# One attention step's scores and keys on one pair of banks, in a fused mLSTM and expert kernel

## The chip, the cores and the metric

The kernel runs on one core of a Trainium2 chip. The metric is the device time of one execution in microseconds (us). TensorE is written PE, VectorE DVE, ScalarE ACT, GpSimd POOL and SyncE SP. Scratch memory of the matmul engine (PSUM) has 8 banks of 512 f32 columns by 128 rows.

## The reference

Four sequences, 8 heads, 768 positions, head size 40. A gated recurrence runs over the positions; its output passes a sigmoid gate, a layer norm and a two-layer network with a residual. All in f32.

```python
for t in range(S):
    m_new = np.maximum(f_gate[:, :, t] + m, i_gate[:, :, t])
    f_stab = np.exp(f_gate[:, :, t] + m - m_new)
    i_stab = np.exp(i_gate[:, :, t] - m_new)
    C = f_stab * C + i_stab * einsum('bhd,bhe->bhde', vt, kt)
    n = f_stab * n + i_stab * kt
    h_tilde = einsum('bhde,bhe->bhd', C, qt)
    denom = np.maximum(np.abs(nq), 1.0)            # nq = n . qt
    y[:, :, t] = sigmoid(o_gate) * h_tilde / denom
x = y as (4, 768, 320)
xn = (x - mean) / sqrt(var + 1e-6) * g_ln
out = x + relu(xn @ w_ch1) @ w_ch2                 # 320 -> 1280 -> 320
```

## The kernel before

The recurrence is computed in chunks of 128 positions. There are 6 chunks (c) of 4 sequences (b), so 24 steps, st = 4c + b; two steps make a pair p, and the expert network works on a pair, 256 positions at once. The program is a list of small pieces, and one long text, `ORDER`, says in which order they are issued: every engine takes its own instructions in that order, and a piece waits on its engine for what it reads and for the buffer or bank that it writes. `@` in the order names the banks of a piece. There is no other scheduler.

The pieces of a step, in the order in which they depend on each other:

- Gates of a chunk: `gm`, `gg`, `gate`, `gu` on DVE and POOL make running maxima, the cumulated log forget gates `gc` and the key-side exponents `uu`. `gst` and `gse` store `gc` and its exponential to DRAM (issued from ACT's queue), `G` and `eg` load them back spread over rows (from SP's queue). `gta`/`gca` and `gr`/`gtr`/`gcr` turn `uu` and its exponential into columns, by a transpose on PE and a copy on DVE.
- Weights of scores: in the first chunk `gx` builds the log weights of a step on PE (mask, then a broadcast of `gc`), and `ex` takes the exponential, one activation per head with the key-side term as bias. In later chunks `sel` masks what `G` loaded, and `ex` does the same.
- `S`: scores of 8 heads. From step 4 on, a chunk is two halves of L = 64 positions, and the score matmuls are 64x64 tiles. `P` multiplies the scores by the weights on DVE.
- `km`, `kv`: weighted keys on POOL, and keys times values on PE, one product per half of the rows, each in a bank of its own. `sd`, `sa`, `se`, `st` carry the state: decay to the middle of the chunk (POOL), plus the first half's product (DVE), decay to its end (POOL), plus the second's (DVE).
- `int`: queries (`qm`) times the state, 64x64 tiles; `pv`: weights times values, added in the same bank, with 64x32 tiles. `n1`, `n2`, `n3`, `sq`, `np`, `nx` normalise and gate on DVE, ACT and POOL; `T`, `xh`, `xl` transpose and split into a high and a low part.
- Expert: `m1.p.f.i` is 8 matmuls of 128x128 weights by 256 columns, `hh` and `hl` split the rectified result, `m2.p.f.j` is 6 matmuls of 320 columns, `ob` and `out` finish and store. f runs over 5 blocks of 256 inner columns. The weights come as 11 tiles: `wl` loads, `cA`, `cB`, `cT`, `cH`, `cL`, `cI` convert and split, `cR` copies half rows.
- `fill` is a matmul into bank 7 that nothing reads.

The first pieces and the way to the first expert matmul in the old order:

```
gin ini id g0 wl.1 wl.0 ld.1 fill.513 fill.513 fill.496 fill.496 fill.496 fill.496 fill.256 fill.256 fill.256 fill.256
fill.320 fill.320 fill.320 fill.320 fill.257 fill.257 fill.257 fill.257 cst ld.0 tok.0 gm.0 wl.2 gg.0 ld.2 gate.0 gu.0
...
fill.512 st.3 fill.512 P.3.1 gex.3 gu.3 kv.2@1 gst.2 P.3.0 fill.512 fill.512 st.2 pv.3 gst.3 sel.5 gm.4 gse.2 gta.3@2
fill.512 n1.3 fill.512 gr.3 gca.3 fill.512 cB.5 n2.3 ex.5.0 gtr.3@6 gcr.3 tok.2 cT.3.0 S.5@0@5 ex.5.1 wl.9 n3.2
m1.0.0.0@1 cT.3.1 nx.2 m1.0.0.1 sq.2 n3.3 cR.3 sd.4 cH.3 P.5.0 T.2@2 fill.512 np.2 nx.3 cI.3@3 gse.3 sel.4 xh.2 hh.0.0
```

Of the kernel before, what the change touches and what calls it, by code (L numbers as in the profile page):

```python
# [20 lines left out]
C = 128  # L21
# [3 lines left out]
VA = 41  # L25
# [11 lines left out]
GP = 4  # L37
NE = 4
# [3 lines left out]
BUFS = {'y': 7, 'xt': 2, 'ht': 4, 'wraw': 4, 'w': 5, 'w0': 2, 'qk': 5, 'wt': 3}  # L42

ORDER = """
gin ini id g0 wl.1 wl.0 ld.1 fill.513 fill.513 fill.496 fill.496 fill.496 fill.496 fill.256 fill.256 fill.256 fill.256
fill.320 fill.320 fill.320 fill.320 fill.257 fill.257 fill.257 fill.257 cst ld.0 tok.0 gm.0 wl.2 gg.0 ld.2 gate.0 gu.0
wl.4 cB.1 cA.1 gm.1 cT.1.0 gg.1 tok.1 cA.0 gta.0@0 gx.1@1@2 gca.0 gr.0 cB.0 gate.1 gex.1 gst.1 g8 cT.1.1 S.1@3@4 gse.1
ex.1.1 cT.0.0 gtr.0@5 wl.3 gx.0@0@6 cT.0.1 gu.1 ex.1.0 P.1.1 cH.1 gcr.0 S.0@1@2 P.1.0 ex.0.0 gm.2 gta.1@4 cI.1@5 gca.1
gg.2 ex.0.1 P.0.0 ld.3 int.1@3@4 pv.1 sig.0 P.0.1 km.1 fill.512 int.0@0@1 cH.0 pv.0 n1.1 km.0 n2.1 n3.1 kv.1@6 wl.5
cB.2 gr.1 gx.3@2@3 n1.0 sq.1 n2.0 nx.1 np.1 kv.0@4 cA.2 n3.0 gx.2@0@1 st.1 ex.3.1 cT.2.0 fill.513 cL.0 st.0 ex.3.0  # L50
cB.4 gtr.1@6 S.2@3@4 nx.0 gate.2 ex.2.0 gcr.1 T.0@2 gu.2 fill.513 ex.2.1 P.2.0 fill.512 fill.512 gex.2 cT.2.1 gta.2@6
km.3 G.5 xh.0 int.2@0@1 fill.513 sq.0 P.2.1 cR.0 fill.512 gr.2 ld.5 gm.3 np.0 int.3@3@4 pv.2 cL.1 cR.2 xl.0 sig.1 eg.2
cB.3 gtr.2@5 gca.2 cH.2 n1.2 T.1@2 G.4 gg.3 kv.3@6 gcr.2 n2.2 xh.1 ld.4 cA.3 S.3@0@5 xl.1 cA.4 fill.512 km.2 gate.3
fill.512 st.3 fill.512 P.3.1 gex.3 gu.3 kv.2@1 gst.2 P.3.0 fill.512 fill.512 st.2 pv.3 gst.3 sel.5 gm.4 gse.2 gta.3@2
fill.512 n1.3 fill.512 gr.3 gca.3 fill.512 cB.5 n2.3 ex.5.0 gtr.3@6 gcr.3 tok.2 cT.3.0 S.5@0@5 ex.5.1 wl.9 n3.2
m1.0.0.0@1 cT.3.1 nx.2 m1.0.0.1 sq.2 n3.3 cR.3 sd.4 cH.3 P.5.0 T.2@2 fill.512 np.2 nx.3 cI.3@3 gse.3 sel.4 xh.2 hh.0.0
fill.512 xl.2 S.4@4@6 sq.3 qm.4 hl.0.0 cL.3 T.3@0 ex.4.0 m1.0.1.0@7 gg.4 xh.3 m1.0.1.1 ex.4.1 xl.3 sd.5 gate.4
m1.1.1.0@5 hh.0.1 P.4.0 np.3 gex.4 sig.2 m1.1.0.0@2 hl.0.1 km.4 gst.4 gse.4 m1.1.1.1 km.5 gu.4 m1.1.0.1 hh.1.1 hl.1.1
kv.4@1@3 hh.1.0 cB.9 gm.5 gta.4@0 gr.4 sa.4 qm.5 hl.1.0 int.4@6@7 gca.4 gtr.4@4 pv.4 se.4 gcr.4 gg.5 st.4 kv.5@1@5
n1.4 n2.4 sa.5 int.5@2@3 cL.2 pv.5 se.5 gate.5 cA.5 cT.4.0 gu.5 gex.5 gst.5 cA.9 st.5 m2.1.0.0@0 n1.5 gse.5 n2.5  # L60
m2.0.0.1@4 cT.4.1 m2.1.0.1@6 cT.5.0 cH.4 wl.6 ld.8 gta.5@7 cT.9.0 m2.0.0.0@1 gr.5 cR.1 cL.4 wl.7 gtr.5@5 ld.6 cT.9.1
m2.0.1.1 G.7 cT.5.1 cH.9 ld.7 m2.1.1.1 gcr.5 n3.4 G.6 cH.5 m2.0.1.0 cL.9 nx.4 wl.8 cL.5 sq.4 cB.6 m2.1.1.0 cA.6 gca.5
# [35 lines left out]
out.5.1 sq.16 ld.21 m1.7.2.1 ld.20 hh.7.0 np.16 ld.23 hl.7.0 out.6.1 T.16@6 sel.20 hh.7.2 m1.7.3.1 xh.16 hl.7.2
m1.7.1.0@7 ex.20.1 xl.16 m2.7.0.0@0 hh.7.3 ex.20.0 hl.7.3 m1.7.1.1 sig.9 m1.7.4.0@1 hh.7.1 sel.22 hl.7.1 m1.7.4.1
kv.17@2@5 ex.22.1 m2.7.0.1@4 km.19 sa.17 ex.22.0 km.18 m2.7.1.1 hh.7.4 hl.7.4 m2.7.1.0 m2.7.2.1 int.17@6@7 pv.17 se.17  # L100
S.22@2@3 qm.19 st.17 n1.17 kv.18@1@5 n2.17 m2.7.2.0 P.22.0 sd.19 sa.18 n3.17 m2.7.3.0 sq.17 int.18@6@7 nx.17 np.17
# [22 lines left out]
def mlstm_moe_kernel(  # L124
# [63 lines left out]
    @piece  # L188
    def g0(_=None):
        nc.sync.dma_start(out=g0_sb, in_=gate0)  # L190
# [659 lines left out]
```

## Time and profile before

| | us |
|---|---|
| median of 3 runs | 339.9 (335.12 to 339.96) |
| the profiled execution | 336.42 |
| its span in the profile | 334.6 |
| PE busy | 317.9 (95%) |
| DVE, ACT, POOL busy | 167.8, 149.8, 133.0 |

The span runs from the first to the last instruction of the program; 1.8 us of the profiled execution lie outside it. Busy time counts overlapping instructions once. Most of PE's matmuls are pipelined: the step from one start to the next is shorter than the time of one.

### The profile page before, as it was taken

What the parts mean: (1) busy time and instruction counts of PE and PEld (TensorE: products, weight loads), DVE (VectorE), ACT (ScalarE), POOL (GpSimd) and SP (SyncE); (2) the same over time, 40 slices, a digit from 0 to 9 for tenths busy, and PEclk for the clock granted to TensorE, in tenths of its full rate; (3) what the DMA queues carried; (4) which work ended last, traced back from release to release, by engine and by line L of the source; (5) the groups of instructions that cost most, each with busy time, mean ns of one, the idle gap of its engine ahead of it and who ended that gap; (6) DMA issues with size and microseconds to landing.
All of it is one profiled execution on the core that took longest, in us unless ns stands there. A gap on an engine that the chain in (4) does not pass through costs nothing.

```text
span 334.6 us, 12179 instructions
## 1 busy us (share of the span) xinstructions
PE 317.9 (95%) x5280; PEld 295.2 (88%) x5280; DVE 167.8 (50%) x419; ACT 149.8 (45%) x411; POOL 133.0 (40%) x221
## 2 busy tenths in 40 slices
PE   7899689999999999999998999999999999999995
PEld 4776577999998998999998899989998999999995
DVE  4778457989744524444441644444444624263221
ACT  2897573568544242236356146228128222252120
POOL 5967196355706321642543355344315423010000
PEclk9999899999999999999999999999999999999999
DMA  7998950698045460049970195355045060000011
GB/s 228 314 318 222 278 165 6 173 348 221 4 120 128 135 209 3 4 145 275 260 167 5 39 205 191 100 194 156 4 130 166 4 202 12 2 24 0 21 41 39
DMA packets 16434, 43.98 MB, mean 131 GB/s; under 512 B 2684, under 2 KB 6012, under 8 KB 16380
## 3 DMA queue, kind: packets, MB, share of 16 engines
q1 hardware_dynamic: 15740, 43.03, 44.4%
q8 instruction: 41, 0.67, 0.8%
q10 hardware_dynamic: 640, 0.16, 0.2%
q14 instruction: 13, 0.11, 0.1%
HBM read 38.44 MB, written 4.10 MB: 127 GB/s over the span
## 4 chain that ended last, share of the span: by engine, by line
PE 69%; DMA 10%; DVE 9%; POOL 4%; issue 3%; ACT 2%; SPq 1%; ACTq 0%; DVEq 0%; POOLq 0%
PE banks L600 27%; PE banks L627 10%; PE banks L628 9%; PE banks L629 9%; DMA wraw<-in_w1a_dram 4%; PE banks L490 4%; PE banks L416 3%; DMA w<-gsc 3%; DMA wraw<-in_w_dram 3%; PE banks L378 2%; PE banks L432 2%; DVE w L386 2%; DVE wt L680 2%; DVE wt L684 1%; PE banks L566 1%
## 5 line engine op out<-in xcount | busy, mean ns | idle before, releaser
L627 PE MATMUL banks<-w2h,hh 128*128 128x320 f32 x240 | 77.2, 322 | 1.8 <-DVE w L386 1.8
L628 PE MATMUL banks<-w2l,hh 128*128 128x320 f32 x240 | 74.2, 309 | 0.8 <-DVE w2l L735 0.8
L629 PE MATMUL banks<-w2h,hl 128*128 128x320 f32 x240 | 73.9, 308 | 0.0
L612 DVE SCALAR_TENSOR_TENSOR hl<-banks,hh 128x512 fp32r<-128x512 f32 x60 | 40.8, 689 | 55.2 <-ACT hh L605 55.1
L600 PE MATMUL banks<-xh,w1h 128*128 128x256 f32 x360 | 63.4, 285 | 1.6 <-DVE w L386 1.5
L600 PE MATMUL banks<-xh,w1l 128*128 128x256 f32 x360 | 61.5, 280 | 0.0
L605 ACT ACTIVATE hh<-banks 128x512 fp32r<-128x512 f32 x60 | 35.1, 592 | 50.8 <-PE banks L600 44.7
L600 PEld LDWEIGHTS banks<-xh,w1h 128*128 128x128 f32 x360 | 51.1, 189 | 3.0 <-DVE w L386 1.4
L600 PEld LDWEIGHTS banks<-xh,w1l 128*128 128x128 f32 x360 | 50.7, 190 | 0.0
L627 PEld LDWEIGHTS banks<-w2h,hh 128*128 128x128 f32 x240 | 45.0, 188 | 4.8 <-DVE w L386 2.5
L600 PE MATMUL banks<-xl,w1h 128*128 128x256 f32 x240 | 47.7, 280 | 1.1 <-issue 1.1
L344 ACT ACTIVATE w<-w,ar_sb 128x64 f32<-128x64 f32 x160 | 40.5, 337 | 13.0 <-POOL w L333 13.0
L628 PEld LDWEIGHTS banks<-w2l,hh 128*128 128x128 f32 x240 | 45.1, 188 | 1.3 <-DVE w2l L735 1.3
L629 PEld LDWEIGHTS banks<-w2h,hl 128*128 128x128 f32 x240 | 45.0, 188 | 0.0
L600 PEld LDWEIGHTS banks<-xl,w1h 128*128 128x128 f32 x240 | 36.8, 190 | 0.0
L392 POOL TENSOR_TENSOR qe<-qk,eg 104x512 f32<-104x512 f32 x20 | 25.6, 1283 | 23.4 <-PE banks L416 12.8
L333 POOL TENSOR_SCALAR_AFFINE_SELECT w<-w 64x512 f32<-64x512 f32 x40 | 28.4, 710 | 12.8 <-DMA w<-gsc 11.0
L634 DVE SCALAR_TENSOR_TENSOR y<-banks,rs,y 128x320 f32<-128x320 f32 x24 | 13.2, 550 | 32.4 <-PE banks L629 32.1
L548 ACT ACTIVATE junk<-y,sum 128x320 bf16<-128x320 f32 x24 | 13.3, 555 | 33.0 <-DVE y L534 33.0
L401 POOL TENSOR_TENSOR kp<-tok,ar_sb 128x320 f32<-128x320 f32 x24 | 16.9, 721 | 26.7 <-issue 9.8
L386 DVE TENSOR_TENSOR w<-banks,w 128x512 f32<-128x512 f32 x28 | 19.0, 688 | 15.1 <-PE banks L378 4.2
L573 ACT ACTIVATE xh<-banks 128x384 fp32r<-128x384 f32 x24 | 11.6, 489 | 32.5 <-PE banks L567 32.5
(101 smaller groups left out, 451.9 us busy)
## 6 DMA issues: line engine op xcount, KB each, us to landing
tok<-in_tok_dram SPq DMA_DIRECT2D x12, 968.0 KB
qk<-in_qk_dram SPq DMA_DIRECT2D x24, 416.0 KB
w<-gsc SPq DMA_DIRECT2D x40, 128.0 KB
out_dram<-y SPq DMA_DIRECT2D x24, 160.0 KB
wraw<-in_w_dram SPq DMA_DIRECT2D x5, 640.0 KB
wraw<-in_w1a_dram SPq DMA_DIRECT2D x5, 512.0 KB
eg<-esc SPq DMA_DIRECT2D x10, 256.0 KB
eg<-esc SPq DMA_DIRECT2D x10, 160.0 KB
```

Source lines behind the costliest of these rows:

```text
L333: nc.gpsimd.affine_select(out=v, in_=v, pattern=[[0, H], [1, L]], compare_op=ALU.is_ge, fill=NEG, base=0, channel_multiplier=-1)
L344: nc.scalar.activation(out=w[:, h], in_=ps[:, hh], func=AF.Exp, bias=ar_sb[:, c, 0, b * H + h:b * H + h + 1])
L386: nc.vector.tensor_tensor(out=w, in0=s_t.pop((st, half)), in1=w, op=ALU.mult)
L392: nc.gpsimd.tensor_tensor(out=t, in0=qk_t[st][:, 0], in1=eg_t[p][:, j], op=ALU.mult)
L401: nc.gpsimd.tensor_tensor(out=kp_t[st][:, :DM].rearrange("p (h e) -> p h e", h=H), in0=kn, in1=ar_sb[:, c, 1, b * H:(b + 1) * H].unsqueeze ...
L490: nc.tensor.matmul(Y[x + i:x + i + 32, h], w[x:x + L, h, i:i + 32], tok_t[p][x:x + L, j, h * VA:(h + 1) * VA], start=False, stop=(g == 3), ...
L600: nc.tensor.matmul(ps[:, i], a, x, start=(n == 0), stop=(n == len(ops) - 1))
L605: nc.scalar.activation(out=t, in_=h1_t[p, f], func=AF.Relu)
L612: nc.vector.scalar_tensor_tensor(out=l.rearrange("p a t -> p (a t)"), in0=ps.rearrange("p a t -> p (a t)"), scalar=0.0, in1=t.rearrange("p ...
L627: nc.tensor.matmul(ps, t[:, i, sl], w2h[:, ff], start=(ff == 0), stop=False)
L628: nc.tensor.matmul(ps, t[:, i, sl], w2l[:, ff], start=False, stop=False)
L629: nc.tensor.matmul(ps, l[:, i, sl], w2h[:, ff], start=False, stop=(ff == KF - 1))
```

## The change

1. From step 4 on, `S` also does the key matmuls of `kv`: scores take columns 0 to 255 of two neighbouring banks, the key products columns from 256 on of the same two. `kv` is left for the first four steps alone.
2. Each sequence has two state tiles, used in turn: `se` and `st` write one, `sd` and `int` of that step read the other.
3. `pv` uses 64x64 tiles instead of 64x32 ones: two matmuls per head, on the two diagonal blocks, instead of four.
4. In the first chunk `gx` adds `uu` on PE too (two matmuls of 64 rows by 512 columns), and `ex` is one activation for four heads without a bias. `gta.0` and `gca.0` go. `gr` writes to a tile `rr` of its own.
5. `gst` and `gse` are issued from SP's queue; the gates come in one load per chunk; `w` has 9 buffers for both kinds of weight tile; 24 of 35 `fill`s go; the order is a new one. `sy` is a DVE copy of one element of `int`'s bank, once.

```diff
+UB = 1
+GA = ()
-BUFS = {'y': 7, 'xt': 2, 'ht': 4, 'wraw': 4, 'w': 5, 'w0': 2, 'qk': 5, 'wt': 3}
+BUFS = {'y': 7, 'xt': 2, 'ht': 4, 'wraw': 4, 'w': 9, 'qk': 5, 'wt': 3}
...
+g0 ini id ld.1 gin.1 cst gin.2 fill.513 fill.513 fill.496 fill.496 fill.496 fill.496 fill.256 fill.256 fill.256
+fill.256 fill.320 ld.0 wl.0 gm.0 wl.1 gg.0 tok.0 gate.0 wl.2 g8 gu.0 ld.3 ld.2 gm.1 gg.1 gx.0@0@1 gate.1 gu.1 gst.1
+wl.3 S.0@2@3 cB.0 ex.0.0 gm.2 gin.3 cA.0 gx.1@0@4 ex.0.1 tok.1 cB.1 cA.1 P.0.1 dg cT.0.0 cT.0.1 S.1@1@3 ex.1.0 cT.1.0
+ex.1.1 gg.2 gx.2@0@5 P.0.0 cH.0 P.1.1 P.1.0 gr.0 cT.1.1 sig.0 cL.0 int.0@6@7 pv.0 ex.2.1 cB.2 cH.1 gtr.0@1 int.1@2@3
+pv.1 cA.2 gcr.0 ex.2.0 gx.3@1@4 n1.1 km.0 n2.1 n1.0 km.1 n2.0 G.5 cT.2.0 wl.5 n3.0 S.3@0@5 ex.3.0 n3.1 ex.3.1 cB.3
+S.2@2@3 gex.1 gate.2 nx.0 gse.1 P.3.0 cA.3 cR.2 gu.2 kv.1@1 P.3.1 sq.1 kv.0@4 nx.1 cT.3.0 gin.4 cR.0 T.0@0 cT.3.1 G.6
+int.3@6@7 cI.1@5 xh.0 cT.2.1 cH.3 wl.4 km.3 pv.3 gm.3 st.1 st.0 xl.0 wl.7 km.2 cL.1 kv.3@1 sq.0 P.2.0 sel.5 T.1@0
+P.2.1 kv.2@4 xh.1 wl.6 cA.5 int.2@2@3 pv.2 gg.3 xl.1 G.4 st.3 sig.1 n1.3 cI.3@5 cR.3 n1.2 cH.2 cR.1 n2.3 cB.5 eg.2
+n2.2 m1.0.0.0@1 n3.2 cL.3 tok.2 n3.3 m1.0.0.1 nx.2 cT.5.0 nx.3 T.2@0 m1.0.1.0@7 hh.0.0 cL.2 ld.4 cB.4 xh.2 hl.0.0
...
-    state = [const.tile([104, 4, VA], F32, name=f"state{b}") for b in range(B)]
+    state = [[const.tile([104, 4, VA], F32, name=f"state{b}_{i}") for i in range(2)] for b in range(B)]
...
     def gst(c):
-        nc.scalar.dma_start(
+        (nc.scalar if c in GA else nc.sync).dma_start(
...
-            nc.scalar.activation(out=u, in_=u, func=AF.Exp, bias=gc[k][0:n, x + m - 1:x + m])
+            nc.scalar.activation(
+                out=rr[k][0:BH, x:x + m], in_=uu[k][0:BH, x:x + m], func=AF.Exp, bias=gc[k][0:BH, x + m - 1:x + m]
+            )
...
+        if st < GP and (UB or st >= B):
+            nc.scalar.activation(out=w, in_=ps, func=AF.Exp)
+            return
...
+        if c or UB:
+            for x in range(0, C, n):
+                for z in range(2):
+                    zs, m, hb = slice(64 * z, 64 * z + 64), slice(x, x + n), 64 * z + b * H + 4 * z
+                    mm(ps[z][m], uu[c % 2][zs, m], id_sb[zs, hb:hb + 4].unsqueeze(2).to_broadcast([64, 4, n]),
+                       start=False, stop=False)
...
+        assert at[1] == at[0] + 1
+        s_t[st, 0] = banks[:, at[0]:at[0] + 2, :4 * L]
+        for g in range(4):
+            for j in range(0, C, L):
+                for z in range(2):
+                    r, m = slice(64 * z, 64 * z + D), slice(j, j + L)
+                    nc.tensor.matmul(
+                        banks[m, at[z], g * L:g * L + L], t[r, 1, g, m], t[r, 0, g, m], start=True, stop=True,
+                        skip_group_check=True
+                    )
+        p, j = divmod(st, 2)
+        kf = kp_t[st]
+        nx = 1 if st >= NST - B else 2
         for g in range(4):
             for z in range(2):
+                h, e = g + 4 * z, (g + 4 * z) * D
+                for x in range(nx):
+                    r, o = slice(L * x, L * x + L), 4 * L + g * VA
                     nc.tensor.matmul(
+                        banks[64 * z:64 * z + 64, at[x], o:o + VA], kf[r, e:e + 64],
+                        tok_t[p][r, j, h * VA:(h + 1) * VA], start=True, stop=True, skip_group_check=True,
                     )
...
     def se(st):
         b = st % B
         p, j = divmod(st, 2)
         nc.gpsimd.tensor_tensor(
-            out=state[b], in0=sa_t[st], in1=eg_t[p][:, j, :, C - 1:C].to_broadcast([104, 4, VA]), op=ALU.mult
+            out=state[b][st // B % 2], in0=sa_t[st], in1=eg_t[p][:, j, :, C - 1:C].to_broadcast([104, 4, VA]), op=ALU.mult
         )
...
     def pv(st):
...
-                    for i in range(0, L, 32):
-                        for x in (0, L):
-                            nc.tensor.matmul(
-                                Y[x + i:x + i + 32, h], w[x:x + L, h, i:i + 32],
-                                tok_t[p][x:x + L, j, h * VA:(h + 1) * VA], start=False, stop=(g == 3),
-                                skip_group_check=True,
-                            )
+                    for x in (0, L):
+                        m = slice(x, x + L)
+                        nc.tensor.matmul(
+                            Y[m, h], w[m, h], tok_t[p][m, j, h * VA:(h + 1) * VA], start=False, stop=(g == 3),
+                            skip_group_check=True,
+                        )
```

## Rows read from the trace of the kernel before

**Rows 1.** The page: engine totals, and the granted clock in 40 slices.

```profile
PE 317.9 (95%) x5280; PEld 295.2 (88%) x5280; DVE 167.8 (50%) x419; ACT 149.8 (45%) x411; POOL 133.0 (40%) x221
...
PEclk9999899999999999999999999999999999999999
```

**Rows 2.** Windows: stretch, length, each engine's busy us, then clock, DMA share, GB/s.

```profile
0.00:30.90 30.90, 28.25 (x326) 19.89 (x327) 20.96 (x62) 22.53 (x63) 21.30 (x44) 1.00 0.92 274
30.90:39.00 8.10, 5.13 (x99) 3.13 (x95) 3.94 (x12) 2.70 (x11) 2.86 (x5) 1.00 0.93 244
39.00:46.30 7.30, 6.27 (x68) 5.45 (x63) 4.20 (x12) 5.70 (x19) 4.76 (x9) 0.77 0.94 287
60.00:86.60 26.60, 26.00 (x280) 24.88 (x278) 23.80 (x41) 18.47 (x46) 13.48 (x19) 1.00 0.80 233
```

**Rows 3.** PE's groups by form, the f32 fills of 512 columns.

```profile
L782 PE MATMUL banks<-id_sb 128*128 128x512 f32 x10 | 7.0, 807 | 1.7 <-POOL id_sb L751 1.7
```

**Rows 4.** Timeline of PE, 38 to 47 us: start, length, what, idle before.

```profile
38.11 0.33 PE L295 MATMUL banks<-id_sb,uu 128*128 128x128 f32 x1 [2.97 <-ACT uu L320]
...
38.99 0.62 PE L600 MATMUL banks<-xh,w1h 128*128 128x256 f32 x3
...
43.35 0.41 PE L566 MATMUL banks<-id_sb,xn 128*128 128x128 f32 x2 [1.03 <-DVE w L386]
...
46.27 0.60 PE L600 MATMUL banks<-xh,w1h 128*128 128x256 f32 x3
```

**Rows 5.** The chain of waits from 100 to 104 us: start, length, what.

```profile
100.14 0.61 PE banks L416 x32
100.75 0.73 PE banks L490 x64
101.48 0.62 PE banks L378 x32
102.10 0.45 PE banks L432 x32
102.55 0.34 PE banks L627
102.89 0.14 PE banks L628
```

**Rows 6.** The same chain: a run of nine `m1`, and `kv` with one half.

```profile
117.99 8.19 PE banks L600 x72
...
259.36 0.46 PE banks L432 x16
```

**Rows 7.** Timeline of ACT, its DMA queue (ACTq) included, 34 to 38 us.

```profile
34.77 0.33 ACTq L281 DMA_DIRECT2D gsc<-gc  x1
...
36.50 0.32 ACTq L281 DMA_DIRECT2D gsc<-gc  x1
...
37.47 0.58 ACT L320 ACTIVATE uu<-uu,gc 32x64 f32<-32x64 f32 x2 [2.02 <-DMA w<-gsc]
```

**Rows 8.** DVE's groups by form: count, busy us, mean ns of one, idle before.

```profile
L386 DVE TENSOR_TENSOR w<-banks,w 128x512 f32<-128x512 f32 x28 | 19.0, 688 | 15.1 <-PE banks L378 4.2 <-PE banks L629 4.2 <-POOL w L333 2.0
L524 DVE SCALAR_TENSOR_TENSOR y<-tok,banks 128x320 f32<-128x320 f32 x24 | 11.4, 479 | 0.0
...
L680 DVE SCALAR_TENSOR_TENSOR wt<-wt,wraw 128x512 int32<-128x512 int32 x5 | 3.9, 795 | 0.0
L684 DVE SCALAR_TENSOR_TENSOR wt<-wraw,wt 128x512 int32<-128x512 int32 x5 | 3.6, 743 | 0.0
L307 DVE COPY ar_sb<-banks 128x32 f32<-128x32 f32 x6 | 1.1, 184 | 1.2 <-PE banks L295 1.2
```

**Rows 9.** Who waited for whom: us in total, times, longest.

```profile
POOL state L466 <- PE banks L416: 25.7, 7, 10.4
PE banks L627 <- DVE w L386: 1.8, 3, 0.8
```

**Rows 10.** Timeline of PE, its last matmul.

```profile
330.82 0.30 PE L629 MATMUL banks<-w2h,hl 128*128 128x320 f32 x1
```

More of the change, by code (lines that the diff above doesn't have):

```diff
@@ L48 @@
[L48 to L62, printed above, removed]
@@ L98 @@
[L98 to L101, printed above, removed]
-pv.18 m2.7.4.0 se.18 n1.18 st.18 n2.18 T.17@2 ob.7.0 m2.7.3.1 xh.17 n3.18 m2.7.4.1 xl.17 sq.18 S.21@1@3 nx.18 np.18
@@ new lines @@
+ld.10 hh.1.4 G.9 st.6 cL.10 int.5@0@1 G.10 gtr.2@7 n3.4 sd.7 m2.0.3.1 gcr.2 hl.1.4 km.7 gta.2@7 pv.5 gca.2 gm.4 qm.6
+S.7@6@7 n1.5 n2.5 n3.5 tok.4 int.6@0@1 eg.4 m2.0.4.1 sa.7 sq.5 se.7 nx.5 m2.0.4.0 ob.0.1 nx.4 st.7 sig.3 T.4@3 P.7.0
+m2.1.4.1 sq.4 sel.10 xh.4 T.5@6 m2.1.3.0 xl.4 xh.5 qm.7 gr.3 xl.5 m2.1.4.0 m1.2.1.0@3 sel.9 pv.6 np.2 int.7@6@7 n1.6
+m1.2.1.1 gg.4 ob.1.0 n2.6 m1.2.2.0@2 hh.2.1 n3.6 m1.2.2.1 gate.4 m1.2.0.0@0 hl.2.1 hh.2.2 gu.4 gst.4 out.0.1
+m1.2.3.0@1 gse.3 np.0 ld.13 ld.11 m1.2.3.1 km.8 ob.0.0 G.13 hl.2.2 qm.8 m1.2.0.1 G.12 S.8@2@3 G.15 hh.2.0 sd.8 ex.9.0
@@ new lines @@
+sel.11 hl.2.0 gin.5 pv.7 G.14 m2.2.0.1@5 ex.9.1 n1.7 np.5 n2.7 ex.10.1 m2.2.1.1 tok.5 sd.9 eg.5 sel.8 m2.2.0.0@0 nx.6
+out.0.0 ex.11.0 m1.2.4.0@6 km.9 hh.2.3 m2.2.1.0 ex.8.0 n3.7 hl.2.3 m2.2.2.1 ex.8.1 m1.2.4.1 sq.6 P.8.0 nx.7 m2.2.2.0
+np.6 gm.5 hh.2.4 gg.5 m2.2.3.1 hl.2.4 sa.8 m2.2.3.0 se.8 m2.2.4.1 np.3 T.6@1 m2.2.4.0 sel.12 ob.1.1 xh.6 ob.2.1 T.7@4
+xl.6 S.9@6@7 xh.7 km.10 st.8 ex.10.0 xl.7 np.4 S.10@1@2 sig.4 ob.2.0 int.8@3@4 P.9.0 m1.3.0.0@5 sd.10 gate.5 qm.9 sa.9
+gst.5 sa.10 m1.3.0.1 out.1.1 ld.12 se.9 m1.3.1.0@0 out.2.0 hh.3.0 se.10 ld.15 gex.5 st.10 out.2.1 m1.3.1.1 hl.3.0 G.19
@@ L189, in g0, with g1, gin @@
     def g0(_=None):
-        nc.sync.dma_start(out=g0_sb, in_=gate0)
+        nc.sync.dma_start(out=g0_sb, in_=gate0[0])
     @piece
-    def gin_(_=None):
-        nc.sync.dma_start(out=gin, in_=gates)
+    def g1(_=None):
+        nc.sync.dma_start(out=g1_sb, in_=gate0[1])
+    @piece
+    def gin(c):
+        gin_t[c] = gin_p.tile([BH, 2, C], F32, tag="gin", name="gin")
+        nc.sync.dma_start(out=gin_t[c], in_=gates[:, :, (c - 1) * C:c * C])
     @piece
@@ L368, in S_ @@
         t = qk_t[st]
-        n = C if st < B else L
-        for z in range(2):
-            s_t[st, z] = banks[:, at[z], :4 * n].rearrange("p (h t) -> p h t", t=n)
-        if st >= B:
-            s_t[st, 0] = banks[:, at[0]:at[1] + 1:at[1] - at[0], :4 * L]
+        if st < B:
+            for z in range(2):
+                s_t[st, z] = banks[:, at[z]].rearrange("p (h t) -> p h t", t=C)
+            for g in range(4):
+                for z in range(2):
+                    r = slice(64 * z, 64 * z + D)
+                    nc.tensor.matmul(
+                        s_t[st, z][:, g], t[r, 1, g], t[r, 0, g], start=True, stop=True, skip_group_check=True
+                    )
+            return
@@ L374, in S_ @@
+        assert at[1] == at[0] + 1
+        s_t[st, 0] = banks[:, at[0]:at[0] + 2, :4 * L]
         for g in range(4):
-            for j in range(0, C, n):
+            for j in range(0, C, L):
                 for z in range(2):
-                    r, m = slice(64 * z, 64 * z + D), slice(j, j + n)
+                    r, m = slice(64 * z, 64 * z + D), slice(j, j + L)
                     nc.tensor.matmul(
-                        banks[m, at[z], g * n:g * n + n], t[r, 1, g, m], t[r, 0, g, m], start=True, stop=True,
+                        banks[m, at[z], g * L:g * L + L], t[r, 1, g, m], t[r, 0, g, m], start=True, stop=True,
@@ L383, in P @@
+        kv_t[st] = [
+            banks[:104, a, 4 * L:4 * L + 4 * VA].rearrange("p (g d) -> p g d", g=4) for a in at[:nx]
+        ]
     @piece
     def P(st, half):
-        w = W_t[st][:, half * 4:half * 4 + 4] if st < B else W_t[st].rearrange("p (z g) t -> p z (g t)", z=2)
+        w = W_t[st][half] if st < B else W_t[st].rearrange("p (z g) t -> p z (g t)", z=2)
         nc.vector.tensor_tensor(out=w, in0=s_t.pop((st, half)), in1=w, op=ALU.mult)
@@ L425, in kv @@
         kf = kp_t[st]
-        if st >= B:
-            for g in range(4):
-                for z in range(2):
-                    h, e = g + 4 * z, (g + 4 * z) * D
-                    for x, a in enumerate((at, at2) if at2 is not None else (at,)):
-                        r = slice(L * x, L * x + L)
-                        nc.tensor.matmul(
-                            banks[64 * z:64 * z + 64, a, g * VA:(g + 1) * VA], kf[r, e:e + 64],
-                            tok_t[p][r, j, h * VA:(h + 1) * VA], start=True, stop=True, skip_group_check=True,
-                        )
-            kv_t[st] = ps, None if at2 is None else banks[:104, at2, :4 * VA].rearrange("p (g d) -> p g d", g=4)
-            return
         n = 64 if st < NE else 32
@@ L474, in st_, with sy @@
         if st < B:
-            nc.scalar.activation(out=state[b], in_=ps, func=AF.Copy)
+            nc.scalar.activation(out=state[b][0], in_=ps, func=AF.Copy)
         else:
-            nc.vector.tensor_tensor(out=state[b], in0=ps[1], in1=state[b], op=ALU.add)
+            s = state[b][st // B % 2]
+            nc.vector.tensor_tensor(out=s, in0=ps[1], in1=s, op=ALU.add)
+    @piece
+    def sy(st):
+        nc.vector.tensor_copy(out=jk_sb, in_=Y_t[st][0:1, 0, 0:1])
     @piece
@@ L769, in ini @@
         nc.gpsimd.memset(uu[1], 0.0)
+        for k in range(2):
+            nc.gpsimd.memset(rr[k], 0.0)
+            nc.gpsimd.memset(gc[k][GR:], 0.0)
         for t in kps:
```

179 lines of the change are left out of this document (96 added, 83 removed).

## The prediction

> **What bounds the kernel now.** I read the page first: TensorE (PE) is busy for 95% of the span, at its full clock except in the fifth of the 40 slices [rows 1]. So nearly every microsecond is PE work or a place where PE waits, and I went on with the windows to see where it waits. From 60 us on PE is busy 26.0 of 26.6 us. From 0 to 39 it is busy too, but much of that is `fill`, matmuls that compute nothing [rows 2, 3]. The timeline shows the one big hole: after 2.97 us without work the transpose `gtr.3` runs at 38.11, the first matmul of the expert part (`m1.0.0.0`) at 38.99, then things stop again, and `m1.0.1.0` starts only at 46.27 [rows 4]. From 39 to 46.3 the mean granted clock is 0.77, a mixture of the 2.4 and 1.2 GHz levels, right behind that idle stretch [rows 2]. The rest of the run is expert matmuls with short attention pieces in between; the chain of waits prices each piece from the end of the one before to its own [rows 5, 6].
>
> Why is the start late? ScalarE computes `gr.3`, the input of `gtr.3`, at 37.47. Its queue is in order, and ahead of `gr.3` stand the DMA issues `gst.2` and `gst.3`, which go out only at 34.77 and 36.50 [rows 7]. DMA is 0.93 busy in these 8 us [rows 2]: the issues wait their turn and hold up arithmetic behind them.
>
> **The change part by part.**
>
> *Gate stores on SP's queue, a new opening.* `gst` and `gse` leave ScalarE's queue, so that this stall cannot recur there. Queued behind them on SP are now loads, `cR.2`, `wl.4` and `wl.7` among them; who waits for those is the weight conversion. The first `m1` stands behind 1 gate transpose instead of 8, no scores of step 5 and 11 fills instead of 33. Its last input is `xl.1` on VectorE. In the old run VectorE is through with `xl.1` at 30.9, with 20.96 us busy until then [rows 2]. The new list up to `xl.1` has 2 more `P` (0.69 each) and 2 more `cT` (0.80, 0.74); one `n1` and `n2` less (about 0.8, 0.48 of it in `n2`) and 5 copies less (0.18 each): +1.4 +1.5 -0.8 -0.9 = +1.2 us [rows 8]. At the old density (20.96/30.9 = 0.68) `xl.1` is done at 30.9 + 1.2/0.68 = 32.7; at the density of 60 to 86.6 (23.80/26.6 = 0.89), counted from about 6 us, where the first gates are through, at 29 to 30 [rows 2]. What PE has in between overlaps for the most part. I put the first `m1` at 33.0 (bounds 30 and 36), against 39.0: the old density, for the two lists are nearly the same.
>
> *First exponents whole, with the key-side term added on TensorE.* `ex` of the first four steps becomes one activation for four; ScalarE gains, but VectorE paces the opening. `gx` gets four more instructions per step, 64 rows by 512 columns in f32, on two halves of the array. The nearest row is the f32 fill of 512 columns, 7.0 us for ten [rows 3]: 0.7 us each, in two rounds 1.4 us per step, 5.6 in four steps; 11.2 if they take turns. Of that same form 6 of the 10 are removed, 4.2 us, and 21 other fills: they are the cover. If PE instead of VectorE paced the opening, this edit would cost its own size less the fills; that is inside the bound of 36.
>
> *Scores and keys together.* `S` now issues the key matmuls right behind the scores, on one pair of banks. Their number stays: 32 + 32 instructions, 0.45 us for the keys where the shape does not change on entry, L432 behind L378 [rows 5]. What changes is how often PE goes from the expert shape (128x128) to the attention shape and back. `int`, 32 instructions too, costs 0.61 as the first piece of a visit, 0.15 more; the first `m2` behind a visit costs 0.34 where the next costs 0.14, 0.20 more. That is 0.35 us a visit. Counted in the two orders from the first `m1` on, there are 34 visits before and 29 after: -5 x 0.35 = -1.8 us.
>
> *Values in 64x64 tiles.* The old `pv`, 64 instructions with 64x32 weights, costs 0.73 us behind `int`, and `S` behind it 0.62 instead of 0.46: a change of shape costs 0.16 each time, so `pv` itself is 0.57 [rows 5]. These changes (22 counted between the two small shapes) vanish: -22 x 0.16 = -3.5 us. But the new `pv` has 32 instructions on only two 64x64 tiles at a time, the diagonal blocks of a head. The trace has a like case: in the last four steps `kv` needs one half of its rows, 16 instructions on two tiles, and takes 0.46 us, as much as 32 instructions on four [rows 5, 6]. A round of two costs what a round of four costs, so the new `pv` is 2 x 0.46 = 0.92 us: +0.35 x 20 = +7.0 us. Bounds: 0.46 (a round holds four, as for `int`) and 1.84 (the two tiles take turns). I take 0.92, from the nearest row. In sum the attention pieces get dearer: -1.8 - 3.5 + 7.0 = +1.7 us.
>
> *Two states per row.* `se` no longer waits until `int` has read the old state. GpSimd waited 25.7 us in seven waits for that [rows 9], but PE's own waits do not name it; I count it at nothing, and what it may cost or give with the waits for banks.
>
> *Waits for banks.* PE waits for VectorE's `P` before `m2`, 1.8 us in three waits [rows 9], because scores hold banks that others need. The merged pair is held longer (until `P`, `sa`, `se` and `st` are done), but a step asks for fewer banks. Counted as PE work between a bank's last writer and its next user against VectorE's in-order work up to the last reader, the old order falls short by 0.8 us or more at five places from step 4 on, the new one at one. I take -2 us (0 to -3).
>
> *The middle.* From the first `m1` to `m2.0.2.0` the new order gives PE and VectorE 16.4 us each, because weight conversion, expert work and the first attention steps come together. Two in-order engines with equal loads do not overlap fully: at the density 0.89 VectorE needs 18.4 us, at 0.68 it needs 24. I take +2 (0 to +6).
>
> **The sum.** The old run, as a check: first `m1` at 39.0; 120 `m1` at 8.19/9 = 0.91 and 120 `m2` at 6 x 0.15 make 217.2 [rows 5, 6]; 19 `S`, 20 `kv` and 20 `int` at 0.46 and 20 `pv` at 0.57, 38.5; 22 `T` at some 0.5 (an estimate from the 0.41 of two of its three matmuls [rows 4]), 11.0; gate transposes and `cI`, 1.5; 34 x 0.35 + 22 x 0.16 = 15.4 for visits and shapes. That ends at 322.6. PE ends at 331.1 [rows 10], so 8.5 us are losses, 3.5 of them in the stop before 46.3; 3.5 us follow to the end of the span, and 1.8 lie outside it. The new run: 33.0 + 217.2 + 20 x (3 x 0.46 + 0.92) = 46.0 + 11.0 + 2.0 + 29 x 0.35 = 10.2 makes 319.4. Losses 8.5 - 3.5 - 2 + 2 = 5.0, tail 3.5, outside 1.8: 329.7 us against the profiled 336.4, -2.0%. The median of the runs shown, 339.9, lies 1.0% above that execution; the same step puts the new median near 332.
>
> **Rivals.** *The values are cheaper (323 us).* If the price went by rounds of four, the new `pv` would take 0.46, and 20 x 0.46 = 9.2 us fall away: 320.5, or 323 at the median. Against it stand the 16 instructions on two tiles that are as slow as 32 on four [rows 5, 6]. By rows, 64 instructions in 0.73 us are 11 ns each. The Trainium skill, "TensorEngine Tiling (Array Packing)", section Instruction Overhead, gives some 60 cycles to each matmul, an estimate of 25 ns at 2.4 GHz, by which halving their number would save 0.8 us per `pv`; the rows lie below that already.
>
> *The opening does not move (340 us).* The first `m1` comes at 36 and the middle costs its full 6 us, because SP, which now also waits for gates, delivers weights late, or VectorE keeps the density 0.68: 3 + 4 = 7 us more than the sum, 336.7, or 340 at the median. For it: DMA is over 0.92 busy throughout the opening [rows 2], and `wl.7` waits for a buffer that a conversion must leave. Against it: `xl.1` was done at 30.9 before.
>
> *Values take turns (351 us, slower).* The diagonal blocks of a head sit in different row halves of the array and write the same bank. If PE ran them one after the other, `pv` would be 1.84, +0.92 x 20 = +18.4 us; the kernel gets slower by over 2% from about +0.7 us per `pv` on. Against it: the old `pv` mixes both row halves in one bank as well, at 11 ns an instruction [rows 5]. The Trainium skill, "TensorEngine Tiling (Array Packing)", section Gotcha 1: PSUM Pressure, says that different row tiles cannot access the same bank at once; by that rule this rival is the outcome, and the rows speak against it.
>
> **Chances.** Forecast 0.52, values cheaper 0.15, opening unmoved 0.25, turns 0.08. Two per cent is about what a measurement of this kernel can tell from no change; seen from 339.9 it ends at 333.1. The forecast's own range is 326 to 338, from the bounds 30 to 36, 0 to +6 and 0 to -3, not all at one end, and is split nearly evenly: 0.29 faster, 0.23 same. The cheaper values give 0.15 to faster; the unmoved opening 0.21 to same and 0.04 to slower; turns 0.08 to slower: faster 0.44, same 0.44, slower 0.12. The range takes in the first two rivals and leaves out the third: 320 to 343.
>
> **What would show it.** First `m1` near 33 in the timeline, no hole of 3 us on PE and the clock at 1.0 between 30 and 50; `pv` at 0.92 us for 32 instructions; keys behind scores at 0.45; 29 visits. I am wrong if `pv` is near 0.5 or above 1.2, if the first `m1` starts after 36, or if PE idles for more than 6 us behind it.

## The result and the profile after

The changed kernel takes 323.09 us (median of 4 runs, 322.38 to 324.59), the kernel before 338.38 in the same session (4 runs, 335.12 to 339.96): a ratio of 0.957, interval 0.948 to 0.966, 4.3% faster. The forecast was 332 (-2.3%): its range of 320 to 343 holds the result, the gain is about twice the forecast. Ratios here leave out the executions that took over 1.5% longer than the fastest of their kernel (a few took 500 to 600 us), medians leave out none unless it is said, so the two can differ. The profiled execution took 322.62 us, with a span of 320.8.

The page of the changed kernel, against [rows 1]: TensorE's (PE's) totals, its granted clock in 40 slices, and the queue that brings instructions (transfers, MB, share).

```profile
PE 312.1 (97%) x4628; PEld 297.6 (93%) x4628; DVE 168.0 (52%) x419; ACT 143.7 (45%) x387; POOL 132.2 (41%) x225
...
PEclk9999999999999999999999999999999999999999
...
q8 instruction: 36, 0.59, 0.8%
```

The same windows as in [rows 2], then two later stretches. The 0.77 of the clock is gone, and from 87 us to its last matmul PE is never idle.

```profile
30.90:39.00 8.10, 7.78 (x78) 7.16 (x78) 7.80 (x21) 6.58 (x16) 4.92 (x7) 1.00 0.93 309
39.00:46.30 7.30, 7.00 (x56) 7.03 (x57) 6.53 (x13) 4.51 (x12) 0.66 (x2) 1.00 1.04 265
...
60.00:87.30 27.30, 26.77 (x472) 25.68 (x473) 20.91 (x50) 12.26 (x34) 15.49 (x24) 1.00 0.63 177
87.30:293.80 206.50, 206.50 (x3269) 201.82 (x3269) 93.31 (x252) 88.39 (x255) 80.08 (x134) 1.00 0.37 107
```

PE's timeline, against [rows 4] and [rows 10]: the first expert matmul starts at 32.99 (before 38.99), the only stop of any size up to 54 us is the 0.62 us before 39.30, and the last matmul starts at 317.19 (before 330.82).

```profile
32.68 0.47 PE L762 MATMUL banks<-w1h,ni_sb 128*128 128x256 f32 x1
32.99 0.51 PE L641 MATMUL banks<-xh,w1h 128*128 128x256 f32 x3
...
39.30 0.59 PE L641 MATMUL banks<-xh,w1h 128*128 128x256 f32 x3 [0.62 <-DVE xh L625]
...
317.19 0.31 PE L670 MATMUL banks<-w2h,hl 128*128 128x320 f32 x1
```

The chain of waits, against [rows 5]: L412 scores, L424 keys, L465 `int`, L532 `pv`, L641 `m1`.

```profile
176.43 0.62 PE banks L412 x32
177.06 0.45 PE banks L424 x32
177.51 0.49 PE banks L412 x32
177.99 0.45 PE banks L424 x32
178.44 0.49 PE banks L465 x32
...
181.90 0.61 PE banks L465 x32
182.51 0.93 PE banks L532 x32
```

All that PE itself waits for from 33 us on (us in total, times, longest). Before, the same list from 46.3 us on held seven entries with 6.4 us: the PE line of [rows 9] and those of the second view.

```profile
PE banks L641 <- DVE xh L625: 0.6, 1, 0.6
PE banks L465 <- DVE t L574: 0.5, 1, 0.5
```

```profile
PE banks L600 <- DVE w L386: 1.5, 3, 0.8
PE banks L600 <- issue: 1.1, 1, 1.1
PE banks L628 <- DVE w2l L735: 0.8, 2, 0.5
PE banks L416 <- DVE sa L460: 0.6, 2, 0.4
PE banks L378 <- DVE w L386: 0.4, 1, 0.4
PE banks L490 <- issue: 0.2, 1, 0.2
```

That list names a wait only where the trace shows a releaser. To count everything I took, for each pair of neighbouring forms of PE instruction, the steps from start to start, and called what a step has over the lower quartile of its pair, if that is more than 60 ns, its excess. What remains is work.

| us | before | after | forecast of the difference | measured |
|---|---|---|---|---|
| first `m1` starts | 39.0 | 33.0 | -6.0 | -6.0 |
| work from there to the last matmul | 273.1 | 275.9 | 286.4 - 283.6 = +2.8 | +2.8 |
| excess | 18.8 | 8.3 | 5.0 - 8.5 = -3.5 | -10.4 |
| last matmul starts | 330.8 | 317.2 | -6.7 | -13.6 |

The excess has two kinds. Small steps of some 0.1 us, most of them where PE goes to attention or comes back, are in both kernels: 84 with 8.1 us before, 75 with 6.8 after. Stops, the steps with over 0.2 us of excess, are what has gone: 16 with 10.7 us before, 2 with 1.5 us after. Nine of the 16, with 6.4 us, ended with a `P` on VectorE (L386). VectorE's load does not explain it: from the first `m1` to the last matmul it is busy 142.2 us before and 142.9 after, in a shorter time.

### The profile page after: what moved, and what is told of

The parts are those of the page before. It is cut to its first block, busy times and chain, and to the rows that moved or that the text cites. A ratio compares the mean times of both kernels' runs of the same rounds, so it can differ in the third digit from the quotient of the medians.

```text
span 320.8 us, 10843 instructions
## 1 busy us (share of the span) xinstructions
PE 312.1 (97%) x4628; PEld 297.6 (93%) x4628; DVE 168.0 (52%) x419; ACT 143.7 (45%) x387; POOL 132.2 (41%) x225
## 3 DMA queue, kind: packets, MB, share of 16 engines
q1 hardware_dynamic: 16732, 43.20, 46.3%
## 4 chain that ended last, share of the span: by engine, by line
PE 94%; DVE 3%; issue 1%; ACT 1%; POOL 1%; DVEq 0%; POOLq 0%
PE banks L641 36%; PE banks L668 12%; PE banks L670 11%; PE banks L669 11%; PE banks L532 6%; PE banks L465 3%; PE banks L412 3%; PE banks L369 3%; PE banks L424 3%; PE banks L829 2%; PE banks L607 2%; PE banks L543 1%; DVE w L435 1%; PE banks L608 1%; DVE mt L253 1%
## 5 line engine op out<-in xcount | busy, mean ns | idle before, releaser
L641 PE MATMUL banks<-xh,w1h 128*128 128x256 f32 x360 | 63.9, 285 | 0.6 <-DVE xh L625 0.6
L641 PE MATMUL banks<-xh,w1l 128*128 128x256 f32 x360 | 61.5, 279 | 0.0
L641 PEld LDWEIGHTS banks<-xh,w1h 128*128 128x128 f32 x360 | 51.5, 188 | 1.7 <-ACT junk L589 0.9
L641 PEld LDWEIGHTS banks<-xh,w1l 128*128 128x128 f32 x360 | 50.5, 187 | 0.0
L641 PE MATMUL banks<-xl,w1h 128*128 128x256 f32 x240 | 47.4, 278 | 0.0
L641 PEld LDWEIGHTS banks<-xl,w1h 128*128 128x128 f32 x240 | 36.5, 188 | 0.0
L340 POOL TENSOR_SCALAR_AFFINE_SELECT w<-w 64x512 f32<-64x512 f32 x40 | 27.5, 689 | 8.2 <-DMA w<-gsc 6.9
L450 POOL TENSOR_TENSOR kp<-tok,ar_sb 128x320 f32<-128x320 f32 x24 | 18.5, 778 | 25.2 <-PE banks L424 10.3
L595 POOL TENSOR_SCALAR rs<-rs 128x1 f32<-128x1 f32 x24 | 4.6, 194 | 57.6 <-ACT junk L589 56.3
L583 ACT ACTIVATE xn<-y,sum 128x320 f32<-128x320 f32 x24 | 13.3, 559 | 24.1 <-DVE y L575 24.1
L532 PE MATMUL banks<-tok,w 64*64 64x41 f32 x640 | 21.8, 228 | 0.0
```

The costliest lines, as they stand in the source:

```text
L340: nc.gpsimd.affine_select(out=v, in_=v, pattern=[[0, H], [1, L]], compare_op=ALU.is_ge, fill=NEG, base=0, channel_multiplier=-1)
L450: nc.gpsimd.tensor_tensor(out=kp_t[st][:, :DM].rearrange("p (h e) -> p h e", h=H), in0=kn, in1=ar_sb[:, c, 1, b * H:(b + 1) * H].unsqueeze ...
L532: nc.tensor.matmul(Y[m, h], w[m, h], tok_t[p][m, j, h * VA:(h + 1) * VA], start=False, stop=(g == 3), skip_group_check=True,)
L583: nc.scalar.activation(out=xn, in_=y_t[st], func=AF.Identity, scale=-float(DM), bias=mu_t[st])
L641: nc.tensor.matmul(ps[:, i], a, x, start=(n == 0), stop=(n == len(ops) - 1))
```

## The experiments

My theory, called 'lead': the shared pair of banks lets the order issue scores and keys well ahead of those who read them, so that PE always has something else to do while VectorE and GpSimd work. In the new order, on average 5.9 of the 8 banks hold something after the first `m1` (old order 4.6). With banks of their own for the keys, its busiest places would need 12. The traces show the lead: over steps 4 to 23, from the end of the last score matmul to `P` it is 0.65 us before and 2.13 after (medians), from the last key matmul to `sa` 0.31 and 1.27, and VectorE sits idle just ahead of `P` and `sa` for 19.7 us in all before, 2.9 after. Rivals: fewer visits to the attention shape, the stores on SP's queue, and the values. ("MoE" in the expectations is the expert part.)

**Scores late, first try.** From step 4 on `S` moves to just ahead of its first reader. To keep the accesses to banks ordered, three one-element copies `sy` ahead of `pv` came with it.

```diff
-... hl.1.2 S.4@0@1 ld.6 ...
+... sa.5 S.4@0@1 P.4.0 ...
...
-S.16@6@7 n1.14 n2.14 sd.17 m1.6.3.1 st.14 tok.9 n3.14 out.5.1 n3.15 ld.18 m2.6.0.0@0 hh.6.3 P.16.0
+n1.14 n2.14 sd.17 m1.6.3.1 st.14 tok.9 n3.14 out.5.1 n3.15 ld.18 m2.6.0.0@0 hh.6.3 S.16@6@7 P.16.0
...
+sy.7 pv.7 ... sy.9 pv.9 ... sy.10 pv.10
```

> The changed kernel with S of step 4 on (scores and keys) moved to just ahead of the first of P and sa, 0 to 7 us of PE work later than in the new order; banks and matmuls as they were, 40 visits instead of 29. Visits alone: +11 x 0.35 = +3.9, 326.5 us. Theory 'lead': most steps lose their lead, PE waits for VectorE again, 5 to 8 us on top, 331 to 335. Rival 'queue': no waits come back, 327 or less.

Measured: 339.77 us (337.24 to 342.0), ratio to before 1.011 (1.000 to 1.022). The whole gain is gone, and PE waits again:

```profile
PE banks L544 <- DVE jk_sb L531: 2.9, 2, 1.5
PE banks L477 <- POOL kp L462: 1.0, 1, 1.0
PE banks L477 <- DVE t L586: 1.0, 1, 1.0
...
```

The first line is PE waiting for added copies, so the run did not say how much is theirs. Two runs took that apart.

**The copies alone.** The changed kernel's order with `sy.7`, `sy.9` and `sy.10` and nothing else.

> The changed kernel with the three one-element copies of scores_late (ahead of the values of steps 7, 9 and 10) and the order otherwise as it was; 29 visits. 'lead': each copy makes TensorE wait some tenths of a us for VectorE: 323 to 326. Rival 'copies': most of the 16 us that scores_late lost is here, 330 or more.

Measured: 324.14 us (323.9 to 324.6), ratio 0.966 (0.956 to 0.976). PE's waits for them:

```profile
...
PE banks L544 <- DVE jk_sb L531: 0.8, 2, 0.4
...
```

The copies by themselves cost 1 us; they are not what took the gain.

**Scores late without copies.** The same move for the 17 steps that need no copy (all from step 4 on but 8, 11 and 12). It was run twice: the first time for its time, the second for its profile.

> The changed kernel, with the scores and keys of 17 of the 20 steps from step 4 on (not 8, 11 and 12) issued just ahead of the first piece that reads them, and no other line changed: none of the one-element copies that scores_late had added. It has 38 visits to the attention shape for 29. Theory 'lead' (the waits of the kernel before have gone because scores and keys are issued well ahead of their readers): 9 visits at 0.25 us give 2.3 us, and TensorE's waits from 33 us on, 1.1 us in the changed kernel, come back to 4 us or more, with the sum of long steps at 14 us or more for 8.3: 328 to 334. Rival 'copies' (scores_late lost its time to the added copies, the lead is worth nothing): visits alone, 324 to 326.5, waits under 2 us.

Measured: 334.1 us, the median of nine of ten executions (330.61 to 335.7; the tenth took 514.26); ratio 0.994 (0.989 to 1.000).

> The kernel of late_no_copies once more, for a profile at the full clock: late_no_copies was 11 us slower than the changed kernel in time, but its profiled execution ran at a granted clock of 0.56. 'lead': TensorE's waits from 33 us on for VectorE, GpSimd or ScalarE, with what queues behind them, make up most of the 11 us (sum of long steps 14 to 18 us for 8.3), 2.3 us are the 9 added visits. Rival 'visits': the sum of long steps stays under 10 us and the visits cost over 0.8 us each.

Measured: 334.15 us for the profiled execution, span 332.4, that is 11.6 over the changed kernel. PE's waits from 33 us on:

```profile
PE banks L544 <- issue: 2.2, 1, 2.2
PE banks L477 <- DVE t L586: 1.0, 1, 1.0
PE banks L477 <- DVE sa L509: 0.7, 1, 0.7
PE banks L314 <- DVE ar_sb L330: 0.6, 1, 0.6
PE banks L653 <- ACT hh L658: 0.6, 1, 0.6
PE banks L477 <- DVE xh L637: 0.6, 1, 0.6
PE banks L477 <- POOL rs L607: 0.6, 1, 0.6
```

By the count of steps the excess goes from 8.3 to 16.6 us: the stops from 1.5 to 7.6 us, the small steps from 6.8 to 9.0. Work grows by 2.3 us for nine more visits, and the first `m1` comes 1.1 later: 8.2 + 2.3 + 1.1 = 11.6 us. The 1.1 is not the edit's: the orders are the same up to there, and in the seven kernels that share this opening and its queue the first `m1` starts anywhere from 32.82 to 34.05. The lead is short again (medians 1.04 us to `P`, 0.51 to `sa`), and VectorE's idle time ahead of them is 19.1 us. 'Lead' holds, with two reservations. 2.4 us of the new stops are the first line, a stop that no other engine causes (below). So 3.7 us are waits for other engines, about half of the 7.2 that the change removed (10.7 less 2.0 of the nameless kind before, less 1.5 after), less than the "most of the 11 us" that I expected. And they are other waits: none of them is for a `P`, as 6.4 us were before; most stand ahead of `int` (L477).

**Keys in a piece of their own.** The key matmuls leave `S` and stand just ahead of `sa`, on the same banks; `sy.9` comes with it.

```diff
+    @piece
+    def ky(st, *at):
         p, j = divmod(st, 2)
         kf = kp_t[st]
...
-sa.5
+ky.5@6@7 sa.5
```

> The changed kernel with the key matmuls of a step in a piece of their own, issued just ahead of sa, on the same banks. Same matmuls, 43 visits of the attention shape instead of 29 after the first expert matmul. If a visit costs 0.35 us, +4.9 us: 327.5. If visits cost nothing and only the banks count, below 324. If the keys' lead over sa is what removed the waits, sa and what hangs on it comes late as well: 330 or more.

Measured: 331.16 us (330.45 to 333.16), ratio 0.985 (0.978 to 0.992). Visits go from 29 to 43 and work from 275.9 to 279.3 us: 0.25 us a visit, where I had put 0.35. The excess grows by 4.4 us, as in the last of the three cases expected (330 or more): late keys are waited for as late scores are.

```profile
PE banks L482 <- DVE t L591: 0.8, 1, 0.8
...
PE banks L482 <- DVE sa L514: 0.4, 1, 0.4
PE banks L426 <- DVE y L582: 0.4, 1, 0.4
...
```

**Values in 64x32 tiles.** Only the third part of the change is undone.

```diff
-                    for x in (0, L):
-                        m = slice(x, x + L)
-                        nc.tensor.matmul(
-                            Y[m, h], w[m, h], tok_t[p][m, j, h * VA:(h + 1) * VA], start=False, stop=(g == 3),
+                    for i in range(0, L, 32):
+                        for x in (0, L):
+                            nc.tensor.matmul(
+                                Y[x + i:x + i + 32, h], w[x:x + L, h, i:i + 32],
+                                tok_t[p][x:x + L, j, h * VA:(h + 1) * VA], start=False, stop=(g == 3),
...
```

> The changed kernel with values in 64x32 tiles again. If a round of tiles costs what the widest weight in it costs (two tiles of 64 columns 0.46 us per 16 instructions), pv falls from 0.92 to 0.57 us in 20 steps, -7.0 us, and 13 changes of tile shape at 0.16 come back, +2.1: 4.9 us less than the changed kernel, 317.7 us against its profiled 322.6. If the price goes by instructions (64 instead of 32), it is 2 us slower than the changed kernel or more, 324.7 or above.

Measured: 322.33 us (320.6 to 323.69), ratio 0.958 (0.952 to 0.963): as fast as the changed kernel. The price was nearly right: summed from start to start, `pv` falls from 0.965 to 0.73 us, and all work from the first `m1` on by 3.9 us, where 4.9 were expected. But stops that no other engine causes took most of it back in the profiled execution, the slowest of the six, in which the first `m1` also comes 0.7 later: PE's waits from 33 us on, then the place of the longest in its timeline, then windows around it, then the queue that brings instructions.

```profile
PE banks L465 <- issue: 1.4, 1, 1.4
PE banks L412 <- issue: 0.9, 2, 0.7
...
PE banks L532 <- issue: 0.2, 1, 0.2
```

```profile
78.39 0.25 PE L465 MATMUL banks<-state,qe 40*64 40x41 f32 x2 [1.39 <-issue]
```

```profile
72.00:79.00 7.00, 5.16 (x203) 4.52 (x203) 4.89 (x16) 2.15 (x6) 4.26 (x6) 1.00 0.41 117
79.00:81.50 2.50, 2.50 (x12) 2.50 (x11) 1.12 (x3) 0.69 (x3) 2.35 (x4) 0.50 0.97 324
```

```profile
q8 instruction: 41, 0.67, 0.9%
```

"issue" means that nothing in the profile releases PE. Counting PE's instructions in the trace, the five stops of over 0.3 us (3.7 us by their steps) all stand at instruction 192 or 193 of a block of 256, and the kernel's 10593 PE records go with 41 transfers of the instruction queue, one per 258. PE waits for its own code: taken in order, one transfer to a block, each of the five stops ends 1.36 to 1.55 us after its block's transfer has landed. Behind the longest stop the granted clock is 0.50 for 2.5 us, the lower of its two levels; a step of `m2` takes 0.27 there for 0.15.

**Values in 64x32 tiles for steps 14 to 23 alone**, to see whether half of them gets the price without the stops.

```diff
+KW = 14
...
+                    n = L if st < KW else 32
+                    for i in range(0, L, n):
...
```

> The changed kernel with values in 64x32 tiles for the last ten steps (14 to 23) and in 64x64 tiles before, so that TensorE has 320 instructions more than the changed kernel and 320 fewer than narrow_values. 'fetch' (64x32 tiles win their 0.23 us a step wherever no stall for instructions comes, and such stalls come where attention steps crowd): 10 x 0.23 = 2.3 us gained less 0 to 2 us of stalls, 320.5 to 323. Rival 'no use' (stalls in long runs of small tiles eat it all): 323 to 325.

Measured: 324.42 us (323.16 to 326.25), ratio 0.964 (0.956 to 0.972): no use. It has two stops for code, again at instruction 193 or 194 of a block:

```profile
PE banks L413 <- issue: 2.4, 2, 1.2
...
```

**Gate stores on ScalarE's queue**, as before the change, in the new order (`GA = (1, 2, 3, 4, 5)` for `GA = ()`).

> The changed kernel with the gate stores gst and gse issued from ScalarE's queue again. Theory 'lead' (PE's waits went because the new order issues scores and keys further ahead of their readers, which the shared banks allow): the queue matters in the opening at most, 322 to 325 us. Rival 'queue' (PE's waits went because DMA issues no longer hold up ScalarE's arithmetic): waits of some 9 us come back, 328 to 333 us, and PE waits for ScalarE in the trace.

Measured: 323.59 us (322.87 to 324.68), ratio 0.962 (0.955 to 0.968). PE's only wait from 33 us on is the 0.5 us for `t`, and the first `m1` starts at 33.85, within the scatter above. In the new order the queue does not matter; this rival falls.

**First exponents per head**, as before the change: `UB = 0`, with `gta.0` and `gca.0` back in the order.

> The changed kernel with the first exponents made as before the change (transposed sums of the first chunk, a copy, and an exponential per head with a bias) in place of whole ones from TensorE. 'opening is set by DMA' (the first MoE matmul waits for the weights that land at some 33 us): first MoE matmul within 0.5 us of 33.0, time 322.5 to 324.5. Rival 'opening is set by the exponents': the eight short ScalarE passes and the longer chain put the first MoE matmul at 35 us or later, time 325 to 329.

Measured: 326.05 us (325.31 to 326.14), ratio 0.972 (0.964 to 0.979). The first `m1` comes 3.3 us later, and from there on the excess is 8.1 us, as in the changed kernel (8.3):

```profile
35.99 0.47 PE L774 MATMUL banks<-w1h,ni_sb 128*128 128x256 f32 x1
36.30 0.51 PE L653 MATMUL banks<-xh,w1h 128*128 128x256 f32 x3
```

**The kernel before, with its gate stores on SP's queue.**

```diff
-        nc.scalar.dma_start(
+        nc.sync.dma_start(
             out=gsc[c]
...
-        nc.scalar.dma_start(out=esc[c] ...
+        nc.sync.dma_start(out=esc[c] ...
```

> The kernel before, with the round trip of the gates (stores and loads of sums and exponents) issued from SyncE in place of ScalarE, as the changed kernel has it, and nothing else. 'queue' (the hole of 2.97 us ahead of the fourth transposition comes from ScalarE's own queue): first MoE matmul at 35.5 to 37 for 39.0, no half clock at 39 to 46: 332 to 336 where the kernel before has 338 to 339. Rival 'order' (the hole comes from the place of the pieces in the order, whatever queue issues): first MoE matmul at 38.5 or later, 337 to 341.

Measured: 334.06 us (331.6 to 337.68, ten runs), before 337.41 in the same session: the medians lie 3.3 us apart, but the ratio, 0.998 (0.993 to 1.004), shows no difference that can be told. Its profile had a granted clock of 0.50 from 12 to 20 us and says nothing of the place of the first `m1`.

> The kernel of old_gates_on_sp once more, for a second profile: in its first one TensorE ran at a granted clock of 0.50 from 12 to 20 us, so that the place of the first MoE matmul (40.7 us) told nothing of the queue. If the round trip's queue made the hole, TensorE's opening at the full clock ends with the first MoE matmul at 35.5 to 37 us; if the order of the pieces made it, at 38.5 us or later. In both, the waits of 46 us and later stay as in the kernel before (TensorE for VectorE's products, 3 us or more), since its order is the old one.

The profiled execution took 609.81 us, and its profile says nothing either; the other took 334.25.

> The kernel of old_gates_on_sp a third time, for its profile alone: the second profile fell in a disturbed execution of 608 us. 'queue': at the full clock the hole of 2.97 us ahead of the fourth transposition is under 1 us and the first MoE matmul stands at 35.5 to 37 us. 'order': the hole is over 2 us and the first MoE matmul stands at 38.5 us or later.

Measured: 335.52 us, span 333.7. PE's timeline, then its waits:

```profile
34.38 0.33 PE L295 MATMUL banks<-id_sb,uu 128*128 128x128 f32 x1
...
36.27 0.62 PE L600 MATMUL banks<-xh,w1h 128*128 128x256 f32 x3
...
39.47 0.41 PE L566 MATMUL banks<-id_sb,xn 128*128 128x128 f32 x2 [1.10 <-ACT w1h L706]
```

```profile
PE banks L378 <- DVE w L386: 1.9, 1, 1.9
PE banks L627 <- DVE w L386: 1.7, 3, 0.8
...
PE banks L600 <- DVE w L386: 1.5, 3, 0.8
```

The hole of [rows 4] is gone and the first `m1` stands 2.7 us earlier: 'queue' holds. But the span of this one execution is only 0.9 shorter: in the old order the excess behind it grows from 18.8 to 20.2 us, with a new wait of 1.9 ahead of scores.

## Why the prediction was right or wrong

*The opening: right in the number, in part by luck.* 33.0 was forecast and measured, but not by the path forecast: `xl.1`, which I had as the last input at 32.7, is done at 31.42, and PE comes to `m1` only behind its own `kv`, `pv` and `cI`, without a stop from 29.52 on. The last line of `xl.1` on VectorE:

```profile
31.13 0.29 DVE L625 TENSOR_TENSOR xh<-banks,xh 64x128 fp32r<-64x128 f32 x1
```

Two runs show what moves the start: SP's queue alone by 2.7 us in the old order (old_gates_third), the whole exponents by 3.3 in the new one (exps_per_head). That these add up to 6.0 is no split, for in the new order the queue moves it by 0.9 at most (gates_on_act). For the exponents my reason was wrong: I had counted them as a cost under the cover of the fills, and they are a gain, since per-head exponents put the first `m1` at 36.3.

*The work: right in the difference, wrong in the level.* `pv` was forecast at 0.92 and takes 0.93 in the chain, 0.965 by its steps; keys behind scores take 0.45 as forecast. That values take turns (1.84) has fallen. The Trainium skill, "TensorEngine Tiling (Array Packing)", section Gotcha 1: PSUM Pressure, would have led there; the row of 0.93 us speaks against it for two blocks on different rows of one bank. Undoing the wide tiles takes 3.9 us off the work, the forecast was 7.0 - 3.5. A visit costs 0.25 in work, not 0.35, and the old order has 33 of them, not 34. In sum +2.8 us forecast, +2.8 measured. The level was too high, 283.6 for 273.1: `T` at 11.0 for 6.4, and attention with its visits at 53.9 for 46.1, part of which stands among the small steps now. One slip is in the arithmetic: 1.0% above 329.7 is 333, not 332.

*The losses: this step failed.* I had 8.5 us of losses in the old run, and 5.0 were to remain: without the 3.5 of the stop before 46.3 (2.6 by the steps), with "-2 us (0 to -3)" for the waits for banks and "+2 (0 to +6)" for the middle. The old run had 10.7 us of stops, 1.5 remain, and the small steps fall by another 1.3: -10.4 for -3.5, nearly the whole error of 7 us. Both terms failed. The middle costs nothing: up to 54 us PE stops once, for 0.8 us. The waits for banks give back far more than 3 us: of 8.7 us of stops for other engines, in the whole of the old run, 7.2 are gone. I had counted the places where a bank's next user comes too early, and how long the merged pair is held, but not how far ahead the order lets PE run, so that VectorE's `P` and `sa` find their inputs ready. Putting the scores late again in 17 steps brings VectorE's idle time ahead of them back in full (19.1 us of 19.7) and about half of PE's 7.2. What removed the waits for `P` is shown by no single run. How the other half of the 7.2 us divides among the remaining moves of the order was not tried; nor was the same order with banks of their own for the keys, which 8 banks don't hold.

*Two states per row* I had put at nothing by itself. GpSimd's old wait for `int` is no longer in the list; it now waits for VectorE's `sa`, 18.3 us in five waits, off PE's path. It was not undone by itself.

*What I had not foreseen:* stops for instructions. Before the change there were three, 2.0 us in excess (at 56.89, 175.21 and 201.16 us); the changed kernel, with 640 matmuls fewer for the values, has none. Fewer matmuls alone do not rule them out, for late_again, with as few, has one of 2.4 us. So the part of the change that I had as a pure cost of 3.5 us about pays for itself.

## What to carry to other kernels

On an engine that is busy for 95%, take the losses from the steps between the starts of its instructions, not as what a sum of single rows leaves over: here a sum that was 4% too high took the losses for less than half of what they were. A change that saves a buffer is worth what order it permits; look in both orders at how many pieces stand between a producer and its reader, at the shortest leads and not at the mean (the first reader is on average the 10th piece behind `S` in the old order, the 11th in the new; but in seven steps of the old it is the 4th or nearer, and in the new never nearer than the 5th), and price the waits that this lead covers. A stop removed from the opening of a fixed order may come back behind it (2.7 us gained, 0.9 kept, in one profile of each), so test it in the order that will run.

## What the runs showed of the hardware

PE can wait for its own instructions. In narrow_values four of the five stops come where the 256 instructions before the border had gone through in 1.4 to 2.7 us, as in a run of attention pieces; but three more borders reached as fast show no stop, the fifth came after 6.6 us, the 2.4 us in late_again after 5.9, and the three of the old kernel after 2.5 to 7.6. In the changed kernel the fastest block takes 3.2 us and none stops. What decides is when the block's transfer of 16 KB lands. In the profiles of before, after, narrow_values, narrow_last and late_again all eleven such stops end 1.20 to 1.61 us after it, and the other 177 borders, which PE reached 1.35 us or more after it, cost at most 0.24 us. Why a transfer comes late is open.
